# ALiBi's key part moved from the exponential's bias into the values, in a kernel of sliding-window attention and a swish feed-forward layer

## Chip, cores, metric

One core of a Trainium2 chip. The metric is device time in microseconds (us), the median of the runs, compared with runs of the kernel before on the same chip in the same rounds. Engines: PE is TensorE (matmul), ACT is ScalarE, DVE is VectorE, POOL is GpSimd, SP is SyncE. SBUF is the on-chip memory of the tiles, PSUM the one that the matmuls write. A run counts as slow when it is over 1.5% above the fastest of its kernel; slow ones are left out of every time and ratio here.

## The reference

```python
# q, k, v: (8 batches, 8 heads, 576 positions, 64); w_in: (512, 2048), w_out: (2048, 512)
scores = scale * np.matmul(q, k.transpose(0, 1, 3, 2))
rel = pos[:, None] - pos[None, :]
bias = slopes[:, None, None] * (-np.abs(rel))          # slopes: 2^-(h+1)
mask = (rel >= 0) & (rel < 128)
scores = np.where(mask, scores + bias[None], -1e9)
attn = softmax(scores)                                  # as exp, sum, divide
x = (attn @ v) as (8*576, 512)
h = x @ w_in
g = h * (1 / (1 + np.exp(-beta * h)))
out = g @ w_out
```

Inside the window the bias is −slope·(query − key). The query part cancels in the softmax, so what remains is a factor exp(slope·key) for each key and head. It can stand in the exponential's bias (before), in the values and in the column of ones that gives the row sum (the change). In 128-blocks of keys it has two versions, one for queries in the key's own block and one for queries in the next block.

## The kernel before

Scores are kept transposed, keys on partitions. In batches 2 to 7 one "visit" (`SC`) covers 1024 columns: two heads by 512. Four exponentials, each with its per-partition bias, one mask product on DVE, and then the PV matmuls (`PV`), whose values come from a tile that POOL casts from fp32.

```python
    def decayed(pt, sps, p, own, w):
        for e in range(2):
            h = 2 * p + e
            for half, cols in ((0, slice(0, own)), (1, slice(own, w))):
                nc.scalar.activation(
                    out=pt[:, e, cols], in_=sps[e][:, cols], func=ACTF.Exp,
                    scale=qscale, bias=bias[:, half, h : h + 1],
                )

    def SC(b, m, p):
        ...                                  # score matmuls into SS, 64 rows
        pt = pt_pool.tile([P, 2, 512], BF16, name="pt", tag="pt")
        decayed(pt, sps, p, OWN[m], 512)
        nc.vector.tensor_tensor(out=pt[:], in0=pt[:], in1=masks[m][:], op=ALU.mult)

    def cast_v(b, sb):                       # one block of values, POOL
        return nc.gpsimd.tensor_copy(
            out=VS[b % 2][0:rows, sb, :, 0:D], in_=fs.pop(("v", b, sb))[0:rows])

    def store():                             # results leave from POOL's queue
        row0, cols, o = waiting.pop(0)
        eng = nc.sync if row0 >= B * S - 2 * P else nc.gpsimd
        eng.dma_start(out=out[row0 : row0 + P, cols], in_=o)

    def Hm(g, j, cs):                        # feed-forward, first layer
        ...                                  # matmuls into hps (two PSUM buffers)
        nc.scalar.activation(out=sig[:], in_=hps, func=ACTF.Tanh, scale=beta_h[:, j : j + 1])
        nc.vector.scalar_tensor_tensor(
            out=gts[g][:, j, :], in0=sig[:], scalar=1.0, in1=hps, op0=ALU.add, op1=ALU.mult)
```

The last line writes gT and with it frees hps. So PE waits for DVE when DVE is late by more than the two hps buffers cover (8 waits, 4.1 us in this kernel's profile). In the traces of this kernel the operations of DVE follow one another, and so do POOL's (two neighbours overlap by at most 0.32 us on DVE and 0.08 on POOL): a mask that takes long delays the gT behind it. POOL carries the casts of q and k, the values, the loads of the weights and the stores.

The softmax here doesn't subtract the row's maximum and nothing guards it: scores larger than these inputs give would overflow.

## Time and profile before

| | kernel before |
|---|---|
| time, median | 339.4 us (338.2 to 340.5, 4 runs) |
| span of the profiled run | 336.8 us, granted PE clock 1.000 |
| mask of 1024 columns: mean, longest | 0.74 us, 1.21 us |
| PE waits over 0.7 us after the first 20 us | 7, together 5.7 us |

The prediction shows the lines of this profile that it used. The timeline: start, duration, engine, line, operation, output and inputs, shapes, count; in brackets the idle time before it and what ended that.

```profile
149.85 0.61 POOL L226 CAST vs<-fst 128x512 bf16<-128x512 f32 x1 [2.75 <-DMA fst<-in_v_dram]
152.02 0.61 POOL L226 CAST vs<-fst 128x512 bf16<-128x512 f32 x1 [1.55 <-DMA fst<-in_v_dram]
...
152.41 0.76 DVE L426 TENSOR_TENSOR pt<-pt,mask 128x1024 bf16<-128x1024 bf16 x1 [0.77 <-ACT pt L319]
...
154.57 0.69 DVE L426 TENSOR_TENSOR pt<-pt,mask 128x1024 bf16<-128x1024 bf16 x1 [0.77 <-ACT pt L319]
```

POOL waits for each tile to land (2.75 and 1.55 us here), so the casts are spread, and each mask finds POOL idle or nearly so (0.76 and 0.69 us).

### The profile page before, as it was taken

How to read it: one execution, taken by the hardware profiler on the slowest of the kernel's cores; microseconds unless marked ns; L12 is line 12 of the kernel's file. 1: busy time of each engine (PE TensorE's matmuls, PEld its weight loads, DVE VectorE, ACT ScalarE, POOL GpSimd, SP SyncE). 2: the span in 40 equal slices, each digit the busy share in tenths (PEclk: the TensorE clock that was granted, in tenths of full speed). 3: DMA queues.
4: the chain of work that ended last, by engine and by line, in shares of the span. 5: the costliest groups of instructions: out<-in, count | busy, mean ns of one | idle time of the engine just before them, and what ended most of it. 6: DMA issues, size and time to landing. Idle time of an engine off the chain costs nothing.

```text
span 336.8 us, 6208 instructions
## 1 busy us (share of the span) xinstructions
PE 320.8 (95%) x2293; PEld 155.4 (46%) x2293; DVE 200.0 (59%) x435; ACT 207.0 (61%) x405; POOL 103.5 (31%) x177
## 2 busy tenths in 40 slices
PE   8889899999998999999999999999999999999995
PEld 4545454444443454444444444444444444444444
DVE  6757897655468883766187717671778167525500
ACT  3767857565538875778469747774878465345511
POOL 4945630428345337321305142322100100010010
PEclk9999999999999999999999999999999999999999
DMA  7999999999999999991939986997120211210022
GB/s 201 241 283 224 168 201 216 202 197 256 215 224 250 176 217 253 219 201 35 219 80 193 186 200 145 214 161 173 45 58 15 78 47 49 55 64 31 0 85 73
DMA packets 146159, 51.81 MB, mean 154 GB/s; under 512 B 135360, under 2 KB 143824, under 8 KB 146128
## 3 DMA queue, kind: packets, MB, share of 16 engines
q1 hardware_dynamic: 139152, 38.29, 61.4%
q0 software_dynamic: 6944, 13.11, 16.4%
q8 instruction: 18, 0.29, 0.4%
q14 instruction: 13, 0.11, 0.1%
q10 hardware_dynamic: 32, 0.01, 0.0%
HBM read 36.71 MB, written 9.44 MB: 137 GB/s over the span
## 4 chain that ended last, share of the span: by engine, by line
PE 73%; DVE 13%; ACT 10%; issue 3%; DVEq 0%; ACTq 0%
PE ops L528 34%; PE hps L502 26%; ACT pt L319 7%; DVE gT L510 4%; PE SS L418 3%; DVE pt L426 3%; ACT sig L509 2%; PE pv L455 2%; PE hpo L502 2%; DVE qkT L252 1%; PE pv L451 1%; PE SS L103 1%; DVE xnp L337 1%; DVE xn L337 1%; PE SS L299 1%
## 5 line engine op out<-in xcount | busy, mean ns | idle before, releaser
L502 PE MATMUL hps<-XT,W 128*128 128x512 bf16 x540 | 135.2, 379 | 4.5 <-DVE gT L510 4.1
L528 PE MATMUL ops<-W,gT 128*128 128x512 bf16 (+1 forms) x592 | 138.5, 374 | 0.5 <-ACT osb L538 0.5
L510 DVE SCALAR_TENSOR_TENSOR gT<-sig,hps 128x512 bf16<-128x512 bf16 x135 | 91.2, 682 | 65.9 <-ACT sig L509 65.2
L509 ACT ACTIVATE sig<-hps,beta_h 128x512 bf16<-128x512 f32 x135 | 92.5, 695 | 56.3 <-PE hps L502 51.6
L319 ACT ACTIVATE pt<-SS,bias 128x256 bf16<-128x256 f32 (+1 forms) x192 | 75.0, 478 | 15.4 <-PE SS L418 15.4
L528 PEld LDWEIGHTS <-gT 128*128 128x128 bf16 x592 | 54.0, 98 | 57.7 <-issue 2.4
L502 PEld LDWEIGHTS <-W 128*128 128x128 bf16 x576 | 51.7, 98 | 60.5 <-issue 9.5
L545 POOL DMA_DIRECT2D out_dram<-osb x34 | 18.4, 542 | 114.0 <-ACT osb L538 113.8
L426 DVE TENSOR_TENSOR pt<-pt,mask 128x1024 bf16<-128x1024 bf16 x48 | 35.6, 742 | 26.6 <-ACT pt L319 26.5
L538 ACT ACTIVATE osb<-ops 128x512 f32<-128x512 f32 (+1 forms) x28 | 16.6, 592 | 38.3 <-PE ops L528 38.3
L226 POOL CAST vs<-fst 128x512 bf16<-128x512 f32 (+1 forms) x40 | 26.0, 657 | 34.3 <-DMA fst<-in_v_dram 31.2
L211 POOL CAST bst<-fst 128x512 bf16<-128x512 f32 (+1 forms) x32 | 20.7, 646 | 49.0 <-DMA fst<-in_q_dram 35.0
L337 DVE TENSOR_TENSOR xn<-pv,zs 128x256 bf16<-128x256 f32 (+1 forms) x62 | 25.9, 421 | 1.6
L212 POOL CAST bst<-fst 128x512 bf16<-128x512 f32 (+1 forms) x32 | 20.6, 644 | 18.1 <-DMA fst<-in_k_dram 17.9
L455 PE MATMUL pv<-vs,pt 128*128 128x65 bf16 x240 | 21.4, 193 | 0.0
L455 PEld LDWEIGHTS <-pt 128*128 128x128 bf16 x240 | 16.5, 97 | 8.4
L418 PE MATMUL SS<-qkT 64*128 64x256 bf16 (+2 forms) x240 | 18.9, 252 | 1.0 <-ACT pt L319 0.8
L418 PEld LDWEIGHTS <-qkT 64*128 64x128 bf16 x240 | 8.2, 94 | 21.2 <-issue 20.7
L451 PE MATMUL pv<-vs,pt 128*128 128x65 bf16 x192 | 17.9, 193 | 0.0
L451 PEld LDWEIGHTS <-pt 128*128 128x128 bf16 x192 | 15.2, 98 | 5.5
L536 DVE TENSOR_SCALAR osb<-ops 128x512 f32<-128x512 f32 (+1 forms) x9 | 5.9, 657 | 18.6 <-PE ops L528 18.5
L336 DVE RECIPROCAL zs<-pv 128x4 f32<-128x4 f32 (+1 forms) x66 | 11.3, 173 | 9.3 <-PE pv L455 8.2
(83 smaller groups left out, 176.5 us busy)
## 6 DMA issues: line engine op xcount, KB each, us to landing
out_dram<-osb POOLq DMA_DIRECT2D x34, 256.0 KB, 3.1
fst<-in_k_dram SPq DMA_DIRECT2D x32, 256.0 KB, 5.1
fst<-in_q_dram SPq DMA_DIRECT2D x32, 256.0 KB, 4.8
fst<-in_v_dram SPq DMA_DIRECT2D x32, 256.0 KB, 4.4
W<-in_moe_w_in_dram POOLq DMA_DIRECT2D x4, 512.0 KB, 7.3
W<-in_moe_w_out_dram POOLq DMA_DIRECT2D x4, 512.0 KB, 10.7
fst<-in_q_dram SPq DMA_DIRECT2D x8, 128.0 KB, 4.1
fst<-in_k_dram SPq DMA_DIRECT2D x8, 128.0 KB, 4.0
```

The source lines that it names most:

```text
L211: nc.gpsimd.tensor_copy(out=t[0:rows, 0], in_=fs.pop(("q", b, sb))[0:rows])
L226: return nc.gpsimd.tensor_copy(out=VS[b % 2][0:rows, sb, :, 0:D], in_=fs.pop(("v", b, sb))[0:rows])
L319: nc.scalar.activation(out=pt[:, e, cols], in_=sps[e][:, cols], func=ACTF.Exp, scale=qscale, bias=bias[:, half, h : h + 1],)
L337: nc.vector.tensor_tensor(out=xn, in0=pv[0:nq, :, 0:D], in1=zs[0:nq].broadcast_to([nq, 4, D]), op=ALU.mult)
L418: nc.tensor.matmul(o, lhsT=qk[64 * e : 64 * e + 64, 1, p, P * kb : P * kb + P], rhs=qk[64 * e : 64 * e + 64, 0, p, P * kb : P * kb + nq], ...
L426: nc.vector.tensor_tensor(out=pt[:], in0=pt[:], in1=masks[m][:], op=ALU.mult)
L451: nc.tensor.matmul(pv[:, hl, 0 : D + 1], lhsT=weights(b, qb - 1, h, 1), rhs=vs[:, qb - 1, h, 0 : D + 1], start=True, stop=False,)
L455: nc.tensor.matmul(pv[:, hl, 0 : D + 1], lhsT=weights(b, qb, h, 0), rhs=vs[:, qb, h, 0 : D + 1], start=qb == 0, stop=True,)
L502: nc.tensor.matmul(hps, lhsT=W1[:, c, bass.ts(j, P)], rhs=XT[:, c, c0 : c0 + TOKG], start=(c == 0), stop=(c == NDM - 1),)
L509: nc.scalar.activation(out=sig[:], in_=hps, func=ACTF.Tanh, scale=beta_h[:, j : j + 1])
L510: nc.vector.scalar_tensor_tensor(out=gts[g][:, j, :], in0=sig[:], scalar=1.0, in1=hps, op0=ALU.add, op1=ALU.mult)
L528: nc.tensor.matmul(ops_[:, cols], lhsT=gT[:, j, i * P : i * P + P], rhs=W2[:, j, cols], start=(j == 0), stop=(j == NFF - 1),)
```

## The change

Its intent: from batch 1 on the factor exp(slope·key) goes into the values. POOL's cast of a value block becomes a product that writes both versions (1024 columns in place of 512), the column of ones gets the factor too, and a visit needs one exponential without bias in place of four. The table matmuls of batch 1 fall away and masks take their place (a third one for the tail); batch 1's q copies go from DVE to ACT, and the mask set-up moves ahead on DVE. The core of the diff:

```diff
 def cast_v(b, sb):
-    return nc.gpsimd.tensor_copy(
-        out=VS[b % 2][0:rows, sb, :, 0:D], in_=fs.pop(("v", b, sb))[0:rows])
+    f = fs.pop(("v", b, sb))
+    if b == 0:
+        return nc.gpsimd.tensor_copy(out=VS0[0:rows, sb, :, 0:D], in_=f[0:rows])
+    x, w, n = f[0:rows], fall[0:rows], 2 if sb < 4 else 1
+    return nc.gpsimd.tensor_tensor(
+        out=VS[b % 2][0:rows, 2 * sb : 2 * sb + n, :, 0:D],
+        in0=bass.AP(tensor=x.tensor, offset=x.offset,
+                    ap=[list(x.ap[0]), [0, n], [D, H], [1, D]]),
+        in1=bass.AP(tensor=w.tensor, offset=w.offset,
+                    ap=[list(w.ap[0]), [H, n], [1, H], [0, D]]),
+        op=ALU.mult)
+
+def values(b, kb, h, then):
+    return VS0[:, kb, h, 0 : D + 1] if b == 0 else VS[b % 2][:, 2 * kb + then, h, 0 : D + 1]
 ...
 def SC(b, m, p):
-    decayed(pt, sps, p, OWN[m], 512)
+    nc.scalar.activation(out=pt[:], in_=SS[:], func=ACTF.Exp, scale=qscale)
     nc.vector.tensor_tensor(out=pt[:], in0=pt[:], in1=masks[m][:], op=ALU.mult)
 ...                      # batch 1 (SP_): the same; no table matmuls; SCT(1): a third mask
-FOUR = {1: 10, 2: 4}
+FOUR = {1: 10, 2: 8}     # hidden tiles that use the other PSUM buffers
 ...                      # set-up: fall = exp(bias), factors into the ones' column, two fills
```

More of the change, by code (lines that the diff above doesn't have):

```diff
@@ L63 @@
     table = const.tile([P, H, 3, P], BF16, name="table")
-    masks = [const.tile([P, 2, 512], BF16, name=f"mask{m}") for m in range(2)]
+    masks = [const.tile([P, 2, 512], BF16, name=f"mask{m}") for m in range(3)]
     kpos = const.tile([P, 1], F32, name="kpos")
@@ L67 @@
     PC = const.tile([P, 1024 + 64], BF16, name="pc")
-    VS = [const.tile([P, NQB, H, D + 2], BF16, name=f"vs{i}") for i in range(2)]
+    fall = const.tile([P, 2, H], F32, name="fall")
+    fallb = const.tile([P, 2, H], BF16, name="fallb")
+    VS0 = const.tile([P, NQB, H, D + 2], BF16, name="vs")
+    VS = [const.tile([P, 2 * NQB - 1, H, D + 2], BF16, name=f"vs{i}") for i in range(2)]
     QK = [const.tile([P, 2, NP, NQB * P], BF16, name=f"qkT{i}") for i in range(2)]
@@ L136, in ones, with padding, falls @@
     def ones():
+        nc.vector.memset(VS0[:, :, :, D : D + 1], 1.0)
+    def padding():
+        nc.gpsimd.memset(VS0[64:P, 4, :, 0:D], 0.0)
         for i in range(2):
-            nc.vector.memset(VS[i][:, :, :, D : D + 1], 1.0)
-    def padding():
-        for i in range(2):
-            nc.gpsimd.memset(VS[i][64:P, 4, :, 0:D], 0.0)
             nc.gpsimd.memset(QK[i][:, :, :, S:], 0.0)
+            nc.gpsimd.memset(VS[1 - i][64:P, 8, :, 0:D], 0.0)
         nc.gpsimd.memset(PC[:, 1024:], 0.0)
-    def biases():
+    def falls():
         for h in range(H):
@@ L152, in biases @@
                 )
+        nc.scalar.activation(out=fallb[:], in_=bias[:], func=ACTF.Exp)
+        nc.vector.tensor_copy(out=fall[:], in_=fallb[:])
+        for i in range(2):
+            w = fallb[:]
+            nc.vector.tensor_copy(
+                out=VS[i][:, 0:8, :, D : D + 1].rearrange("k (n a) h d -> k n (a h d)", a=2),
+                in_=bass.AP(tensor=w.tensor, offset=w.offset,
+                            ap=[list(w.ap[0]), [0, 4], [1, 2 * H]]))
+            nc.vector.tensor_copy(
+                out=VS[i][:, 8, :, D : D + 1].rearrange("k h d -> k (h d)"), in_=w[:, 0])
     def betas():
@@ L176, in tail_masks @@
         fill(1, 384, 1, P, ALU.is_lt)
+        fill(2, 0, 4, 64, ALU.is_ge)
+        fill(2, 256, 4, 64, ALU.is_lt)
     fs = {}
@@ L251, in TP @@
                     tok[:, c], lhsT=src[:, i, c], rhs=ident[:], start=True, stop=True)
-            (nc.vector.tensor_copy if b or i else nc.scalar.copy)(
+            (nc.vector.tensor_copy if i else nc.scalar.copy)(
                 out=QK[b % 2][:, i, p, 0:FULL], in_=tps[:])
@@ L270 @@
              "B": ((1, 256, 256, P), (2, 0, 256, 256), (3, 128, 384, P))}
-    PLAIN = ((1, "B"),)
     WIDTH = {"A": 384, "B": 512}
@@ L277, in SP_ @@
         w = WIDTH[vis]
-        plain = (b, vis) in PLAIN
+        plain = b == 1
         for e in range(2):
@@ L305, in SP_ @@
         pts[b, vis, p] = pt
-        if not plain:
-            nc.scalar.activation(
-                out=pt[:, :, 0:w], in_=sps[:, :, 0:w], func=ACTF.Exp, scale=qscale)
-            return
-        decayed(pt, [sps[:, e] for e in range(2)], p, 256, w)
-        nc.vector.tensor_tensor(
-            out=pt[:, :, 0:w], in0=pt[:, :, 0:w], in1=masks[0][:, :, 0:w], op=ALU.mult)
-    def decayed(pt, sps, p, own, w):
-        for e in range(2):
-            h = 2 * p + e
-            for half, cols in ((0, slice(0, own)), (1, slice(own, w))):
-                nc.scalar.activation(
-                    out=pt[:, e, cols], in_=sps[e][:, cols], func=ACTF.Exp,
-                    scale=qscale, bias=bias[:, half, h : h + 1],
-                )
+        nc.scalar.activation(out=pt[:, :, 0:w], in_=sps[:, :, 0:w], func=ACTF.Exp, scale=qscale)
+        if plain:
+            nc.vector.tensor_tensor(
+                out=pt[:, :, 0:w], in0=pt[:, :, 0:w], in1=masks[0][:, :, 0:w], op=ALU.mult)
     def room(b, shape, i):
@@ L340, in PVP @@
     def PVP(b, vis, p):
-        vs = VS[b % 2]
         if vis == "A":
@@ L353, in PVP @@
                         pv[:, 2 * n + e, 0 : D + 1], lhsT=pt[:, e, at : at + P],
-                        rhs=vs[:, kb, 2 * p + e, 0 : D + 1],
+                        rhs=values(b, kb, 2 * p + e, int(kb < q0 + n)),
                         start=i == 0, stop=i == len(ws) - 1,
@@ L369, in SCT @@
         for e in range(2):
+            if b:
+                break
             t = table[:, e]
@@ L381, in SCT @@
                         rhs=qk[64 * e : 64 * e + 64, 0, p, FULL:S],
-                        start=False, stop=True, skip_group_check=True,
+                        start=b > 0, stop=True, skip_group_check=True,
                     )
@@ L386, in SCT @@
             scale=qscale)
+        if b:
+            nc.vector.tensor_tensor(
+                out=PC[:, 0:1024], in0=PC[:, 0:1024],
+                in1=masks[2][:].rearrange("p e w -> p (e w)"), op=ALU.mult)
     def DT(b, sb):
@@ L401 @@
     COLS = {0: (0, 384), 1: (128, 256), 2: (0, 384), 3: (192, 320), 4: (128, None)}
-    OWN = (256, 320)
     def SC(b, m, p):
@@ L406, in SC @@
         qk = QK[b % 2]
-        sps = [SS[:, e] for e in range(2)]
         for kb in ((0, 1), (2, 4, 3))[m]:
@@ L411, in SC @@
             for e in range(2):
-                o = sps[e][:, at : at + min(nq, 512 - at)]
+                o = SS[:, e, at : at + min(nq, 512 - at)]
                 if kb in (0, 2):
@@ L439, in PV @@
         nq = ROWS[qb]
-        vs = VS[b % 2]
         if g == 0:
@@ L452, in PV @@
                     pv[:, hl, 0 : D + 1], lhsT=weights(b, qb - 1, h, 1),
-                    rhs=vs[:, qb - 1, h, 0 : D + 1], start=True, stop=False,
+                    rhs=values(b, qb - 1, h, 1), start=True, stop=False,
                 )
@@ L456, in PV @@
                 pv[:, hl, 0 : D + 1], lhsT=weights(b, qb, h, 0),
-                rhs=vs[:, qb, h, 0 : D + 1], start=qb == 0, stop=True,
+                rhs=values(b, qb, h, 0), start=qb == 0, stop=True,
             )
@@ L689, in tail_casts @@
             cast_v(b, 4)
+        falls()
+        constants_masks()
+        tail_masks()
         after(get_pair(1, 0), w1[0])
@@ L752, in open_o @@
                 tc.tile_pool(name="psum_o", bufs=2, space=bass.MemoryType.PSUM))
-        steps = [h[2], biases, constants_masks, h[3], R(0), h[4], A(0), h[5], B_(0), R(1), h[6],
+        steps = [h[2], h[3], R(0), h[4], A(0), h[5], B_(0), R(1), h[6],
                  A(1), B_(1), R(2), h[7], A(2), R(3), B_(2), A(3), h[8], B_(3), open_o, VA(0),
-                 h[9], VA(1), h[10], VA(2), tail_masks, lambda: TT(0), h[11], VA(3),
+                 h[9], VA(1), h[10], VA(2), lambda: TT(0), h[11], VA(3),
                  lambda: SCT(0), VB(0), h[12], VB(1), lambda: PV(0, 4, 0), VB(2), h[13], XO(0),
```

## The prediction

"Lock" stands in it for what the trace of the kernel before shows: a mask that begins inside a cast on POOL ends late. Of the 18 such masks 16 ended 0.54 to 0.64 us after the cast; the one at 168.46 ended 1.10 us after its cast and 0.55 after the next, and one in batch 1 (40.97) 0.94 us after. How long a product takes on POOL no trace had shown yet: the prediction's +5 to +8 us for DVE and its 150 us for POOL rest on an estimate of mine.

> **What bounds the kernel now.** I read the page's busy times and slices first, then the groups of instructions, then the waits, then the timeline round the places where TensorE (PE) stands still.
>
> ```profile
> PE 320.8 (95%) x2293; PEld 155.4 (46%) x2293; DVE 200.0 (59%) x435; ACT 207.0 (61%) x405; POOL 103.5 (31%) x177
> ...
> DVE gT L510 <- ACT sig L509: 67.2, 68, 7.7
> ACT sig L509 <- PE hps L502: 51.6, 81, 5.8
> ...
> PE hps L502 <- DVE gT L510: 4.1, 8, 0.8
> ...
> L319 ACT ACTIVATE pt<-SS,bias 128x256 bf16<-128x256 f32 (+1 forms) x192 | 75.0, 478 | 15.4 <-PE SS L418 15.4
> L426 DVE TENSOR_TENSOR pt<-pt,mask 128x1024 bf16<-128x1024 bf16 x48 | 35.6, 742 | 26.6 <-ACT pt L319 26.5
> L226 POOL CAST vs<-fst 128x512 bf16<-128x512 f32 (+1 forms) x40 | 26.0, 657 | 34.3 <-DMA fst<-in_v_dram 31.2
> L307 ACT ACTIVATE pt<-SX 128x1024 bf16<-128x1024 f32 x4 | 4.1, 1024 | 0.2
> L288 PE MATMUL SS<-table,ident 128*128 128x384 bf16 x16 | 4.0, 335 | 0.0
> ```
>
> The first line: PE is busy 95% of 336.8 us, ACT and DVE some 60%, so work taken from ACT is worth only what PE waits for it. Busy PE time hides short stalls (ends are modelled), so I went through the starts of the matmuls in the timeline. Two dense 128x512 matmuls start 216 ns apart, and a switch to or from the 64-row score matmuls costs about 95 ns more; what exceeds that I call stall. It sums to 22 us: 7.4 in the first 20 us, 5.0 from 20 to 40, 1.2 from 40 to 60 and about 8.6 from 60 to the end, 0.7 of it in the drain. The last 280 us are thus within 3% of what this order of matmuls allows. The waits say the same: PE waits for gT 8 times, 4.1 us together. The group lines give the costs used below. One such stall in the timeline:
>
> ```profile
> 166.87 1.56 ACT L319 ACTIVATE pt<-SS,bias 128x256 bf16<-128x256 f32 x4
> ...
> 167.95 0.61 POOL L211 CAST bst<-fst 128x512 bf16<-128x512 f32 x1
> ...
> 168.46 1.21 DVE L426 TENSOR_TENSOR pt<-pt,mask 128x1024 bf16<-128x1024 bf16 x1 [0.77 <-ACT pt L319]
> ...
> 168.51 0.61 POOL L212 CAST bst<-fst 128x512 bf16<-128x512 f32 x1
> ...
> 169.59 0.68 DVE L510 SCALAR_TENSOR_TENSOR gT<-sig,hps 128x512 bf16<-128x512 bf16 x1
> ...
> 170.32 1.02 PE L502 MATMUL hps<-XT,W 128*128 128x512 bf16 x4 [0.57 <-DVE gT L510]
> ```
>
> Four exponentials hold ACT for 1.56 us, the mask behind them takes 1.21 us instead of 0.69 because two casts on POOL lie over it, gT comes late, and PE waits for the PSUM buffer that gT frees. Nine stalls over 0.4 us, some 6.2 us together, stand between 104 and 281 us. Four of them (147.6, 169.6, 215.3, 223.3) follow a mask that took 0.97 to 1.21 us, that is, one that a POOL cast held up.
>
> [...]undisturbed masks take 0.69 us, and each one that starts inside a cast ends about 0.55 us after that cast. gT (one input in PSUM) stays at 0.68 us beside casts.
>
> **The change part by part.**
>
> *Exponentials.* The 48 visits of batches 2 to 7 have four ACTIVATEs each, 75.0 us / 48 = 1.56 us; one of 1024 columns takes 1.02. ACT saves 0.54 x 48 = 26 us, and another 0.54 x 4 = 2 us in batch 1. Four q copies of batch 1 move from DVE to ACT: +4 x 0.585 = +2.3 us. ACT goes from 207 to about 181 us. Nearly all of this lies beside PE work. On the path: each of the nine late stalls can shrink by at most the 0.54 us by which exp, and the tanh behind it, end earlier. The two at 104.4 and 107.7 (1.4 us) lie where the change also gives four more hidden tiles of group 2 another PSUM buffer. I take -4.0 us of the 6.2 for both together, before what POOL does.
>
> *PE.* The table matmuls go in batch 1: 4 visits x 2 of 384 columns and 2 of 512, at 216 ns per 512: 8 x 0.162 + 2 x 0.216 = 1.7 us. PE is the bound there, so all of it counts: -1.7 us. The 2283 matmuls left are the same. Of the qkT waits in batch 1 (0.42, 0.27 and 0.55 us of stall at 27.5, 31.7 and 36.6) the split of the copies over two engines takes perhaps half: -0.6 us. With the table matmuls gone, less work covers the rest.
>
> *DVE.* Off: 4 q copies of 0.685 = 2.7 us. On: 4 masks of 768 columns at about 0.55 us, one 1024-column mask for the tail at 0.69, five small copies (about 0.5) and two more mask fills (2 x 0.28). Busy time stays at 200 to 202 us plus what POOL blocks. But place matters: the order of instructions puts the small copies ahead of the second k copy of batch 0, and the fills ahead of the reciprocal and beta_h behind it. In the chain of the kernel before, these places are on the path (masks 7.98, qkT 9.20, zs 11.38, beta_h 12.02, PE 12.15). I count +1.0 us at the start.
>
> *POOL.* [...]It has idle time, so that is not the bound. It hurts in two ways. First the lock: I laid the products into the POOL timeline of before (each where its v tile had landed, the next behind it) and looked which masks start inside one. The delay of DVE comes to 9.7 us if DVE gets its turn between two POOL operations and 13.1 if it does not, against 4.7 and 5.3 with a length of 1.1 us: +5 to +8 us of DVE delay. In the stalls above, some half of a mask's delay reached PE: +2.5 to +4, I take +3.0. Second, the products of batch 1 stand before the W2 loads and batch 2's casts: W2's later loads go out some 3 us later, and batch 2's transposes wait for the last. The third of these landed at 70.9 us and the score matmuls that need it start at 71.1, so there is no slack: +0.5 us, with the chance of 2. Later batches have 4 us or more of slack for the values.
>
> The sum: -4.0 - 1.7 - 0.6 + 1.0 + 3.0 + 0.5 = -1.8 us. On 339.3 that is 337.5; the times of before scatter by 1.2 us each way. Since shorter exponentials also start the masks earlier, which helps in front of a POOL product that has not begun, I put it at 337.0.
>
> **The rivals.** (a) *ACT relief is worth more:* the nine stalls and the waits of batch 1 all vanish because one exponential frees the score tile and ACT together, and POOL's products turn out short (cast-like, about 1.2 us). Then -6.2 - 1.7 - 1.5 + 1.0 = -8.4: 331. For it: the waits name ACT's sig in 65 us of DVE's idle time. Against it: PE itself stalls for 8 us only, and the two-input operation reads twice as much. (b) *POOL takes the place of ACT:* the products run back to back, DVE's masks starve behind them for several us at a time, gT is late in every batch and PE stalls 1.5 us or more per batch: +9 on top, 346. For it: at 168.46 the second cast kept the lock although the mask had been waiting. Against it: v tiles land about 2 us apart, and only some 8 masks come per batch. (c) *Nothing moves:* all of ACT's saving lies beside PE, only the table matmuls count, and the start takes them back: 338 to 339.
>
> **Range and chances.** PE's work sets a floor: with all stalls after 20 us gone except those inherent to the small transposes, some 326 us, which nobody should expect. Rivals (a) and (b) mark the ends; I give each about one in ten. Predicted 337.0 us, range 331.5 to 343.0. Faster by over 2% (under 332.5) 0.13, slower by over 2% (over 346) 0.05, within 0.82.
>
> **What would show it.** Right: ACT near 181 us, 2283 matmuls, POOL near 150 us[...], masks (two SBUF inputs) lengthened to 1.5 us and more where they start inside a product, first 20 us about 1 us later at the same instruction, stalls of PE after 60 us no more than 2 us below before. Wrong: products near 1.2 us (the POOL term falls away and (a) gains), masks starved for over 3 us (b), or PE waiting at the first scores of batch 2 for over 1 us. If the time falls by more than 6 us, I have undervalued the relief of ACT on the path to gT; if it rises by more than 4, I have undervalued the lock.

## The result, and the profile after

The changed kernel takes 358.78 us (355.21 to 360.37, 4 runs) against 339.37: a ratio of 1.056, 95% interval 1.047 to 1.065. It is slower by 19 us, far outside the predicted range. Ratios here and below are the mean time of one kernel's runs over that of the other's of the same rounds, so they are not quite the ratio of the medians that I quote.

The page of the changed kernel, first the busy times, then the granted PE clock in 40 slices (tenths of full speed), then three groups (busy time, mean ns of one, idle time before them and what ended it):

```profile
PE 325.2 (91%) x2283; PEld 155.6 (44%) x2283; DVE 227.4 (64%) x442; ACT 182.7 (51%) x254; POOL 146.1 (41%) x178
...
PEclk9999989999998999995999999999989999999999
...
L445 DVE TENSOR_TENSOR pt<-pt,mask 128x1024 bf16<-128x1024 bf16 x48 | 56.7, 1181 | 23.1 <-ACT pt L444 23.0
...
L247 POOL TENSOR_TENSOR vs<-fst,fall 128x1024 bf16<-128x1024 f32 (+1 forms) x35 | 63.3, 1822 | 13.1 <-DMA fst<-in_v_dram 12.7
...
L444 ACT ACTIVATE pt<-SS 128x1024 bf16<-128x1024 f32 x48 | 48.9, 1019 | 22.9 <-PE SS L437 22.9
```

ACT is relieved as intended (207 to 183 us). But the mask, the same instruction as before, takes 1181 ns on average in place of 742. The waits of the changed kernel (engine, what it waited for; us in total, times, longest) say where it reaches PE:

```profile
POOL vs L247 <- DMA fst<-in_v_dram: 12.7, 11, 3.1
PE hps L520 <- DVE gT L528: 11.1, 4, 6.9
...
PE pv L469 <- DVE xn L353: 4.1, 2, 3.2
...
PE tpt L291 <- DVE xnp L353: 4.0, 1, 4.0
```

PE waited 4.1 us for gT before, in 8 waits of at most 0.8; now 11.1 us in 4 waits, the longest 6.9. The two other long waits of PE, for xn (3.2 us) and xnp (4.0 us), are also for DVE results that stood behind a long mask (5.14 us at 105.23, 4.91 us at 40.28). For a value tile PE hardly waits (0.2 us in all). The first line is a sign of the bunching below: POOL waited for value tiles 19 times, 31.2 us before, now 11 times, 12.7 us, so more tiles lie ready when POOL gets to them. The timeline of the longest stall:

```profile
154.25 0.54 POOL L563 DMA_DIRECT2D out_dram<-osb  x1 [7.08 <-ACT osb L556]
154.81 7.47 POOL L247 TENSOR_TENSOR vs<-fst,fall 128x1024 bf16<-128x1024 f32 x4
154.90 7.93 DVE L445 TENSOR_TENSOR pt<-pt,mask 128x1024 bf16<-128x1024 bf16 x1 [1.00 <-ACT pt L444]
156.31 0.29 PE L473 MATMUL pv<-vs,pt 128*128 128x65 bf16 x4
162.76 0.67 DVE L528 SCALAR_TENSOR_TENSOR gT<-sig,hps 128x512 bf16<-128x512 bf16 x1
163.48 3.57 PE L520 MATMUL hps<-XT,W 128*128 128x512 bf16 x8 [6.88 <-DVE gT L528]
```

Read it from the top. A store at the head of POOL's queue waits 7.08 us for its data; meanwhile four value tiles land. Then the four products run back to back for 7.47 us. The mask starts 0.09 us after the first and ends at 162.83, that is 0.55 us after the last product (162.28): it stood through all four. gT comes behind it, and PE has stood for 6.88 us. At a second place a mask stood through two products and the DMA issue on POOL between them, and ended 0.60 us after the second:

```profile
40.02 1.91 POOL L247 TENSOR_TENSOR vs<-fst,fall 128x1024 bf16<-128x1024 f32 x1
40.28 4.91 DVE L337 TENSOR_TENSOR pt<-pt,mask 128x1024 bf16<-128x1024 bf16 x1
41.86 0.80 POOL L267 DMA_DIRECT2D W<-in_moe_w_out_dram  x1
42.68 1.91 POOL L247 TENSOR_TENSOR vs<-fst,fall 128x1024 bf16<-128x1024 f32 x1
```

Not every mask that met a run stood through it. Four others in this trace (76.82, 78.97, 81.50 and 130.32; 1.19 to 1.51 us) ended 0.55 us after the product in which they had begun, though the next product had started 0.04 us before that end. The next product was then the longer one: 2.35 us at 77.48 and at 79.79 in place of 1.90, and 1.48 to 1.49 at 82.10 and 131.24 (64 rows) in place of 1.05.

There is a second cost that I had not thought of. The windows of the changed kernel (stretch; its length, busy time and number of instructions of PE, PEld, DVE, ACT, POOL; granted PE clock, DMA share, GB/s):

```profile
152.00:156.00 4.00, 4.00 (x28) 1.82 (x26) 2.48 (x3) 3.26 (x5) 1.73 (x2) 1.00 0.38 111
...
160.00:164.00 4.00, 0.52 (x2) 0.24 (x2) 4.00 (x4) 0.00 (x0) 2.27 (x2) 0.50 0.00 0
164.00:168.00 4.00, 4.00 (x16) 1.24 (x15) 1.82 (x6) 1.59 (x3) 0.00 (x0) 0.50 0.21 44
```

After the stall the granted PE clock is 0.50: the eight hps matmuls at 163.48 take 3.57 us, while eight took 1.90 at 153.58. Windows at or near 0.50 follow each of the four stalls of over 3 us in this trace (41.5: 4.05 us; 108.0: 3.38; 156.4: 7.05; 253.7: 3.24). In windows of 1 us, PE's busy time times (1 − clock) sums to 7.8 us here and to 0.0 in the kernel before. That is the most that the half clock can have cost in matmuls. By the starts of the matmuls, the stretches at half clock run 6.5 us over the full pace; part of it is won back elsewhere (the net is in the sum further down).

### The profile page after: what moved, and what is told of

It reads as the page before. It is cut to its first block, busy times and chain, and to the rows that moved or that the text cites.

```text
span 356.6 us, 6044 instructions
## 1 busy us (share of the span) xinstructions
PE 325.2 (91%) x2283; PEld 155.6 (44%) x2283; DVE 227.4 (64%) x442; ACT 182.7 (51%) x254; POOL 146.1 (41%) x178
## 4 chain that ended last, share of the span: by engine, by line
PE 76%; DVE 15%; ACT 5%; issue 2%; DVEq 0%; ACTq 0%
PE ops L546 34%; PE hps L520 28%; DVE pt L445 6%; PE SS L437 4%; DVE gT L528 3%; ACT pt L444 2%; DVE pt L337 2%; PE pv L473 2%; PE hpo L520 2%; PE pv L469 1%; PE SS L106 1%; ACT sig L527 1%; ACT pt L335 1%; PE tps L280 1%; DVE xnp L353 1%
## 5 line engine op out<-in xcount | busy, mean ns | idle before, releaser
L520 PE MATMUL hps<-XT,W 128*128 128x512 bf16 x532 | 136.1, 387 | 11.2 <-DVE gT L528 11.1
L546 PE MATMUL ops<-W,gT 128*128 128x512 bf16 (+1 forms) x592 | 140.2, 377 | 1.4 <-DVE osb L554 0.9
L527 ACT ACTIVATE sig<-hps,beta_h 128x512 bf16<-128x512 f32 x133 | 91.4, 688 | 86.5 <-PE hps L520 74.0
L445 DVE TENSOR_TENSOR pt<-pt,mask 128x1024 bf16<-128x1024 bf16 x48 | 56.7, 1181 | 23.1 <-ACT pt L444 23.0
L247 POOL TENSOR_TENSOR vs<-fst,fall 128x1024 bf16<-128x1024 f32 (+1 forms) x35 | 63.3, 1822 | 13.1 <-DMA fst<-in_v_dram 12.7
L444 ACT ACTIVATE pt<-SS 128x1024 bf16<-128x1024 f32 x48 | 48.9, 1019 | 22.9 <-PE SS L437 22.9
L229 POOL CAST bst<-fst 128x512 bf16<-128x512 f32 (+1 forms) x32 | 21.2, 663 | 11.6 <-DMA fst<-in_k_dram 11.6
L469 PE MATMUL pv<-vs,pt 128*128 128x65 bf16 x192 | 18.3, 194 | 4.1 <-DVE xn L353 4.1
L473 PE MATMUL pv<-vs,pt 128*128 128x65 bf16 x240 | 21.8, 195 | 0.0
L437 PEld LDWEIGHTS <-qkT 64*128 64x128 bf16 x240 | 8.1, 95 | 21.6 <-issue 21.2
L235 POOL CAST bst<-fst 128x512 bf16<-128x512 f32 x16 | 10.0, 640 | 6.8 <-PE xtp L378 3.6
```

The lines of the kernel that those rows point to most:

```text
L229: return nc.gpsimd.tensor_copy(out=t[0:rows, 1], in_=fs.pop(("k", b, sb))[0:rows])
L247: return nc.gpsimd.tensor_tensor(out=VS[b % 2][0:rows, 2 * sb : 2 * sb + n, :, 0:D], in0=bass.AP(tensor=x.tensor, offset=x.offset, ap=[lis ...
L437: nc.tensor.matmul(o, lhsT=qk[64 * e : 64 * e + 64, 1, p, P * kb : P * kb + P], rhs=qk[64 * e : 64 * e + 64, 0, p, P * kb : P * kb + nq], ...
L444: nc.scalar.activation(out=pt[:], in_=SS[:], func=ACTF.Exp, scale=qscale)
L469: nc.tensor.matmul(pv[:, hl, 0 : D + 1], lhsT=weights(b, qb - 1, h, 1), rhs=values(b, qb - 1, h, 1), start=True, stop=False,)
L473: nc.tensor.matmul(pv[:, hl, 0 : D + 1], lhsT=weights(b, qb, h, 0), rhs=values(b, qb, h, 0), start=qb == 0, stop=True,)
```

## The experiments

Theory L (lock): a mask, two inputs from SBUF, that begins inside a POOL operation with an input from SBUF does not end before it, and may be held on through the next ones if they follow without a gap (7.93 us above); so the loss is a matter of how long POOL's runs of reading operations are. Rival R1: POOL's time as such, values late for PV, or the rest of the change (start, other PSUM buffers, batch 1). Rival R2: the size of one product alone counts, the lock falling at each end of an instruction. Seventeen kernels ran.

| run | what | time, us | ratio to before [95%] |
|---|---|---|---|
| e1_cast_only | after, plain cast of V (wrong result) | 335.08 | 0.992 [0.988, 0.996] |
| e2_before_products | before, products by 1 on POOL | 354.99 | 1.049 [1.044, 1.053] |
| e7_reduce | after, mask replaced by a one-input DVE operation (wrong) | 344.66 | 1.017 [1.013, 1.021] |
| e4_split | after, each product in two halves | 351.17 | 1.036 [1.029, 1.043] |
| e3_one_input | after, copies in place of products (wrong) | 341.53 | 1.002 [0.995, 1.009] |
| e6_dve_product | after, products on DVE | 367.28 | 1.082 [1.075, 1.088] |
| e5_act_store | after, stores from ACT's queue | 349.42 | 1.029 [1.024, 1.033] |
| e12_before_act_store | before, stores from ACT's queue | 352.17 | 1.039 [1.035, 1.044] |
| e14_gap_memset | after, memsets ahead of each product | 346.96 | 1.024 [1.021, 1.027] |
| e15_turns | after, each product waits for the mask before it | 344.28 | 1.014 [1.008, 1.020] |
| e18_turns_gap | e15, and e14's memsets in batch 1 | 341.10 | 1.005 [1.001, 1.009] |
| e8_fold | factor in the masks, plain V | 342.52 | 1.012 [1.010, 1.014] |
| e10_fold_pool | e8, set-up on POOL | 361.78 | 1.066 [1.062, 1.070] |
| e11_fold_pool_act_store | e10, stores from ACT's queue | 366.87 | 1.081 [1.078, 1.085] |
| e13_fold_late | before to batch 1, folded from batch 2 | 342.47 | 1.011 [1.009, 1.013] |
| e16_fold_spread | e13, set-up spread | 334.90 | 0.989 [0.986, 0.992] |
| e17_fold_turns | e16, and V casts wait for the mask before them | 334.49 | 0.987 [0.984, 0.990] |

### Take the products away, and add them alone (e1, e2)

```diff
 # e1: the changed kernel
-    x, w, n = ...;  return nc.gpsimd.tensor_tensor(out=VS[b % 2][... both versions ...], ...)
+    return nc.gpsimd.tensor_copy(out=VS[b % 2][0:rows, 2 * sb, :, 0:D], in_=f[0:rows])
 # e2: the kernel before, from batch 1 on
-    return nc.gpsimd.tensor_copy(out=VS[b % 2][0:rows, sb, :, 0:D], in_=...)
+    ... the changed kernel's product with two versions, by a tile of ones
```

> The changed kernel with the cast of the values on POOL as before (one version, unscaled, read for both uses): wrong result on purpose, everything else as changed. Theory L[...]: without products the masks go back to about 0.74 us on average and the time falls to 333 to 336 us, a little below before, since one exponential per visit and 1.7 us of table matmuls remain as gains. Theory S (the loss is in the new set-up work, the order of DVE's first instructions, and the masks added in batch 1): stays at 350 us or more. Theory E (one long exponential in place of four makes ACT or the score tile worse): stays at 350 or more, with long waits on ACT.

> The kernel before with only the products added: each v cast of batches 1 to 7 becomes the same two-version product on POOL, with factors of one, so the result stays right; exponentials with bias, tables and set-up stay as before. Theory L: slower than before by about what the changed kernel lost to masks, 352 to 362 us, with masks of 4 us and more and PE stalls of 3 us and more right after them. Theories S and E: 338 to 341 us, as before.

Measured: e1 335.08 us, 0.8% faster than before, with the wrong values. e2 354.99 us, 4.9% slower than before, with a right result and with all four exponentials, tables and PSUM buffers of before (from two runs; its profiled run was slow). So the product on POOL alone makes the loss, and everything else in the change is worth about −3 us. That dismisses the second half of R1. The group lines of e1's page:

```profile
L438 DVE TENSOR_TENSOR pt<-pt,mask 128x1024 bf16<-128x1024 bf16 x48 | 39.3, 820 | 25.4 <-ACT pt L437 25.1
...
L246 POOL CAST vs<-fst 128x512 bf16<-128x512 f32 (+1 forms) x35 | 23.5, 676 | 36.2 <-DMA fst<-in_v_dram 29.6
```

With the cast back, the masks are at 820 ns, and POOL waits for value tiles for 29.6 us again, as before the change.

### A DVE operation with one input (e7)

```diff
-    nc.vector.tensor_tensor(out=pt[:], in0=pt[:], in1=masks[m][:], op=ALU.mult)
+    nc.vector.tensor_reduce(out=pt[:, 0, 0:1], in_=pt[:].rearrange("p e w -> p (e w)"),
+                            op=ALU.max, axis=mybir.AxisListType.X)
```

> The changed kernel with each of the 48 mask products of batches 2 to 7 replaced by a reduction of the same 1024 columns on DVE, which has one SBUF input (wrong result on purpose). It is longer by itself[...]. POOL's products stay. Theory L, by the two SBUF inputs of the mask: none of these 48 is stretched by POOL, stalls of over 3 us after 60 us are gone, and the time falls to 340 to 347 us in spite of the longer instruction (batch 1's masks still starve). A rival, load: DVE and POOL simply have too much to do; then the time rises above 359.

Measured: 344.66 us. From its page:

```profile
L445 DVE TENSOR_REDUCE pt<-pt 128x1 bf16<-128x1024 bf16 x48 | 58.6, 1221 | 18.8 <-ACT pt L444 18.3
...
L247 POOL TENSOR_TENSOR vs<-fst,fall 128x1024 bf16<-128x1024 f32 (+1 forms) x35 | 60.6, 1744 | 15.9 <-DMA fst<-in_v_dram 15.5
```

The products are all there, and they do not touch the reductions: the 31 that overlap a reading POOL operation take 1.20 to 1.22 us, the 17 others 1.22. DVE is as busy as in the changed kernel (227.8 against 227.4 us), since the reduction is slower than an undisturbed mask (1.22 against 0.69 us). And yet no stall of PE after 60 us is over 1.3 us, where the changed kernel has three over 3. So what does the harm is the mask meeting POOL's operations, not DVE's busy time and not late values, which dismisses the first half of R1. The reduction differs from the mask in two ways, one input and hardly any output; that it is the input, against POOL's reads, is my reading of two more facts: gT, which writes 512 columns but reads one input from SBUF, takes 0.65 to 0.69 us in the changed kernel beside a reading POOL operation (57 cases) as elsewhere, and in e14 a mask goes on beside POOL operations that only write. (Its 2.5 us stall at 43.7 falls in batch 1, whose eight masks I had left as they were.)

### Half-size products, and one-input copies (e4, e3)

```diff
 # e4
-    nc.gpsimd.tensor_tensor(out=both versions, in0=x twice, in1=w, op=ALU.mult)   # 1024 columns
+    for n in range(2 if sb < 4 else 1):
+        r = nc.gpsimd.tensor_tensor(out=version n, in0=x, in1=w[n], op=ALU.mult)  # 512 columns
 # e3
+    nc.gpsimd.tensor_copy(out=both versions, in_=x twice)
```

> The changed kernel with each two-version product as two one-version products (about 1.05 us each, right result). If DVE gets its turn at the end of each POOL instruction, the longest wait of a mask is halved and the time falls to 345 to 352 us. If a mask goes on waiting as long as POOL's next instruction is ready (starvation, what the 4.9 to 7.9 us masks of the changed kernel suggest), nothing is gained: 354 to 364 us, with masks of 5 us and more.

> The changed kernel with each product on POOL replaced by a copy that reads the v tile twice and writes the same 1024 columns (one input, wrong result on purpose). Estimate from the 0.61 us of a 512-column cast: 1.1 to 1.2 us instead of 1.9. If the runs of POOL work are what starves the masks, shorter instructions leave more gaps between the arrivals of v tiles: masks stretched to 3 us at most, 338 to 346 us. If only two-input instructions on POOL lock the masks out: as with the plain cast, 333 to 336 us. If the length does not matter but the number of columns written does: 355 or more.

e4: 351.17 us, inside what was expected if the lock falls at the end of each instruction, so by its time alone e4 would speak for R2. The timeline of e4 decides otherwise:

```profile
149.62 6.03 POOL L248 TENSOR_TENSOR vs<-fst,fall 128x512 bf16<-128x512 f32 x6
...
149.71 6.49 DVE L445 TENSOR_TENSOR pt<-pt,mask 128x1024 bf16<-128x1024 bf16 x1 [1.00 <-ACT pt L444]
```

Six products of about 1 us, one mask through all six; it ends at 156.20, 0.55 us after the sixth. Here the ends of five products did not free the mask, which dismisses R2 with its lock that falls at each end. What e4 gains lies elsewhere: the stall at 108 us is gone, the longest falls from 7.05 to 5.61 us, and the one at 41.5 us from 4.05 to 2.06, where a mask that began at 40.49 ended at 43.41, 1.14 us after a product, while the next one ran; between the two lay a DMA issue (42.20 to 43.01), and that the mask got in during it is my reading. e3: 341.53 us (wrong; its profiled run slow). The copy of 1024 columns takes 1.07 us on average in place of 1.98, and the time is that of before within the interval. Its longest mask was still 4.42 us, across a run of four copies. So products, copies and casts (168.46 in the kernel before) have all held masks, and what differs is how long the runs last.

### Somewhere else for the product, and for the stores (e6, e5, e12)

```diff
 # e6
-    return nc.gpsimd.tensor_tensor(out=VS[b % 2]...
+    return nc.vector.tensor_tensor(out=VS[b % 2]...
 # e5 (changed kernel) and e12 (kernel before)
-    eng = nc.sync if row0 >= B * S - 2 * P else nc.gpsimd
+    eng = nc.sync if row0 >= B * S - 2 * P else nc.scalar
```

> The changed kernel with the products on DVE itself, in order with the masks (right result). [...]DVE's busy time goes from about 200 (without blocks) to 235 to 240 us, POOL has no v work from batch 1 on. Theory L: no mask stands behind POOL products; but products delay gT by 1.2 us in DVE's order: 338 to 346 us. Load as the cause: 355 or more.

> The changed kernel with the stores of the result issued from ACT's queue and not POOL's (right result). In the changed kernel the longest run of products (154.8 to 162.3 us) began when a store at POOL's head, waiting for its output tile, let go, with the v tiles long landed. If such bunching makes the longest runs, the stalls of 7.0 us at 156 and 3.2 us at 254 shrink to under 1.5 us and the time falls by 7 to 12 us, to 346 to 352. If the products bunch anyway (POOL too slow for v tiles 2 us apart): 355 to 360.

> The kernel before with the stores on ACT's queue alone, as a control for the run of the changed kernel with ACT stores, which gained 9 us. With casts of 0.6 us bunching costs little: 336 to 340 us, within 1% of before. If stores on POOL were costly by themselves, it would gain the same 9 us: 330. Right result.

e6 missed: 367.28 us, worse than the changed kernel; by its expectation that would mean load, but the trace shows waiting. A product, 1.23 us on average on DVE, waits there for its tile: 19.9 us in 11 waits for the V tiles, up to 7.9 us, in which neither masks nor gT go on. DVE's busy time is 239.0 us. The run does not speak on the lock. e5: 349.42 us, 9 us less than the changed kernel; the stalls at 156 and 254 us, each behind a store at POOL's head, are gone, those at 40 and 109 us remain. That supports the reading of the bunching. But e12, the control, missed: the same move costs the kernel before 13 us (one stall of 6.4 us at 78.4; DVE waits up to 6.9 us for an exponential, and that ACT held it behind stores whose data were not ready is my reading, not shown). So e5's 9 us is a net figure, and moving the stores is no cure.

### Give the mask a gap, or a turn (e14, e15, e18)

If a next operation that is always ready is the harm, then a gap, or a wait that gives DVE its turn, must cure it with all the work left in place.

```diff
 # e14: ahead of each product (e18: in batch 1 only)
+    for _ in range(6):
+        nc.gpsimd.memset(scrap[:], 0.0)          # 128 columns; reads no SBUF
 # e15, e18: the product waits for the mask issued last before it
+    if "mask" in late:
+        after(r, late["mask"])                   # a dependency
 ...
-    nc.vector.tensor_tensor(out=pt[:], in0=pt[:], in1=masks[m][:], op=ALU.mult)
+    late["mask"] = nc.vector.tensor_tensor(out=pt[:], in0=pt[:], in1=masks[m][:], op=ALU.mult)
```

> The changed kernel, with six small memsets of 128 columns on GpSimd ahead of each V product from the second batch on: GpSimd operations that read no tensor in SBUF, as a gap of some 0.5 us or more between two products. Correct result expected. Lock with no gap (the mask needs one moment in which no GpSimd operation is reading, and gets none while the next product is ready): the longest masks end within the gap after the product that they met, so no mask over 2.0 + 0.7 = 2.7 us, against 7.93 in the changed kernel, the stalls of over 3 us fall to under 2, time 342 to 352. Plain loss of bandwidth while GpSimd is busy with anything, or a grant that only the emptying of GpSimd's queue gives: masks stay at 5 us or more, time 357 to 364.

> The changed kernel, with each V product made to wait for the mask that was issued last before it in the program's order, so that DVE gets a turn before each product; all else equal, the same work. Correct result expected. Starvation by a product that is always ready: masks of over 3 us vanish except where two products follow the same mask, the stalls of over 3 us after 40 us go with them, time 338 to 347. If the time is lost in GpSimd's busy time itself (4 us of work more in each batch, whatever its order), the wait only moves it: 355 to 362. If the wait delays products until PV matmuls stand for V: 350 to 370, with PE waits on vs in place of gT.

> e15 (each V product waits for the mask issued last before it), and in the second batch alone the six memsets of e14 ahead of each product, because there two products wait for the same mask and the second starved one mask in e15 (5.47 us at 39.6, stall 4.67 us, half clock after it). Correct result expected. If that one stall is most of what e15 still lost: it vanishes, no mask over 3 us in the second batch, 337 to 341. If the wait for masks itself costs the rest: 343 to 345 as in e15.

e14: 346.96 us with 43 us of memsets on top (POOL is busy for 185 us against 146), with a right result. Its timeline:

```profile
159.50 1.53 POOL L249 MEMSET scrap<- 128x128 bf16 x6
161.00 1.90 POOL L250 TENSOR_TENSOR vs<-fst,fall 128x1024 bf16<-128x1024 f32 x1
161.57 1.88 DVE L448 TENSOR_TENSOR pt<-pt,mask 128x1024 bf16<-128x1024 bf16 x1 [0.23 <-ACT pt L447]
162.84 1.51 POOL L249 MEMSET scrap<- 128x128 bf16 x6
```

The mask meets the product, and ends at 163.45, 0.55 us after it (162.90), in the middle of the memsets. The longest mask is 3.07 us, at 89.12, a little over the 2.7 that I had expected; it stands in a run of q and k casts, which have no memsets between them. What e14 still loses is partly POOL's delay: its largest stall, 4.4 us at 126.9, waits for qkT, the transposed q and k of the next batch, whose casts presumably come late behind the longer products.

e15: 344.28 us, three quarters of the loss gone with the same work as the changed kernel and a few waits more. At the place of the 7.93 us mask its timeline has

```profile
154.85 0.54 POOL L566 DMA_DIRECT2D out_dram<-osb  x1 [5.39 <-ACT osb L559]
155.50 0.69 DVE L448 TENSOR_TENSOR pt<-pt,mask 128x1024 bf16<-128x1024 bf16 x1 [1.00 <-ACT pt L447]
156.33 3.76 POOL L247 TENSOR_TENSOR vs<-fst,fall 128x1024 bf16<-128x1024 f32 x2 [0.94 <-PE pv L476]
```

The store comes late as before, but the mask goes first, in 0.69 us, and the products follow. One stall of 4.67 us was left, at 41.0, where a mask of 5.47 us stood through two products of batch 1 that wait for the same earlier mask; the wait cannot part those. e18 puts memsets there as well: the stall is gone, no mask is over 3 us (the longest is 2.96, in a run of casts at 87), and the time is 341.10 us, at the edge of the expected 337 to 341. Of the 5.6% loss 5.1 points are undone by turns and gaps, with every product still on POOL.

### The factor in the masks (e8, e10, e11, e13, e16, e17)

This asks whether the gain of the exponentials can be had without a product on POOL. The factor of a key is multiplied into the mask, so there are eight masks (two kinds by four pairs of heads) in place of two; V stays a plain cast. It costs 32 small DVE operations once.

```diff
 # e13, e16, e17: the kernel before up to batch 1; from batch 2 on
+    def folded(m, p, j):
+        own = (256, 320)[m]
+        for e in range(2):
+            for half, cols in ((0, slice(0, own)), (1, slice(own, 512))):
+                r = nc.vector.tensor_scalar_mul(
+                    FM[m][p][:, e, cols], masks[m][:, e, cols],
+                    fall[:, half, 2 * p + e : 2 * p + e + 1])
+                after(r, ...)                    # not before a given gT (m = 0)
 ...
-        decayed(pt, sps, p, OWN[m], 512)
-        nc.vector.tensor_tensor(out=pt[:], in0=pt[:], in1=masks[m][:], op=ALU.mult)
+        nc.scalar.activation(out=pt[:], in_=SS[:], func=ACTF.Exp, scale=qscale)
+        nc.vector.tensor_tensor(out=pt[:], in0=pt[:], in1=FM[m][p][:], op=ALU.mult)
 # e16: the second set built pair by pair, behind the first four masks of batch 2
+        if (b, m) == (2, 0):
+            folded(1, p, None)
 # e17: cast_v also waits for the last mask, as the product in e15
 # e8: folded from batch 1 on, all set-up on DVE; e10: that set-up on POOL;
 # e11: e10 with the stores from ACT's queue
```

> A way to the change's aim without products: ALiBi's key part is multiplied into the 0/1 masks once, one mask per pair of heads, so the visit keeps one exponential and one mask product, no tables from batch 1 on, and the values are cast as before. Right result. Theory L: masks at about 0.74 us, 332 to 336 us. About 48 small DVE instructions at the start may cost 1 to 2 us of that. Theory E: 345 or more.

> The kernel with the key part folded into the masks, but with the set-up of masks and factors moved from DVE to POOL, in program order where POOL waited for DMA (after the paddings, after batch 1's first v casts, and ahead of batch 2's casts). In the first fold kernel the set-up stood ahead of qkT copies, beta_h and the reciprocals on DVE and PE stalled 18.5 us in the first 40 us against 12.4 in the kernel before; after 60 us it stalled about 4.7 us against 8. If only the place of the set-up spoilt it: first 40 us at 11 to 12 us of stall, 329 to 333 us, faster than before by 2 to 3%. If the small POOL instructions delay the q and k casts instead: 335 or more. Right result.

> The same with the stores of the result on ACT's queue. If a store waiting at POOL's head still bunches casts (masks of 1 us and more behind casts): 1 to 2 us less than the same kernel with stores on POOL. If the issue of stores costs ACT as much: the same within 1 us. Right result.

> The kernel before up to batch 1, tables and all; from batch 2 on the key part is folded into the masks (one exponential and one mask product per visit, plain values, casts on POOL as before). The 32 small instructions that build the folded masks are held back on DVE until the last gT tiles of the second token group, where DVE had idle time, so the start is that of before. If only the place of the set-up spoilt the first two fold kernels: stalls of the first 60 us as before (about 13 us), after that about 5 against 8.8, and 3 to 5 us less in all: 334 to 336.5 us, ratio 0.985 to 0.992. If the building delays gT around 66 to 76 us: 337 to 340. Right result.

> The kernel before up to the second batch, from the third batch the key part folded into eight sets of masks (no product on GpSimd, one exponential and one mask per visit), as e13, but the set-up of the second set is spread, one pair of heads behind each of the masks of the third batch, in place of one run of twelve operations at 77 us. Correct result expected. If e13's 1.1% loss was its bunched set-up (4.2 us of PE stall at 77 us): 334 to 339, ratio 0.985 to 1.0. If a run of four V casts on GpSimd that starves the masks is what is left: 339 to 342 with masks of 2.5 to 3 us at 90 and 154 us.

> e16 with each V cast made to wait for the mask issued last before it. Correct result expected. If runs of casts starve masks there: 1 to 2 us less than e16 and no mask over 2 us after 80 us. If those long masks cost PE nothing: the same as e16 within 0.5 us.

e8 (342.52 us) and e13 (342.47) are 1% slower than before, though no product is on POOL: e8 builds its masks in the first 60 us, where DVE is on the path, and e13 has twelve of the set-up operations in one run at 77 us, in front of an eviction that PE waits 4.2 us for. e10 and e11 missed badly (361.78, 366.87): POOL took about 1 us for a `tensor_scalar` of some 256 columns with a per-partition factor (mean of the 24 of one group 954 ns), its casts came late behind them, and PE stood for 8.3 and 10.6 us. e16 spreads the set-up and gives 334.90, with no stall over 1.1 us after 20 us; e17's waits add nothing that shows (334.49; the intervals overlap). From e17's page:

```profile
PE 317.8 (95%) x2253; PEld 155.2 (47%) x2293; DVE 209.5 (63%) x467; ACT 183.1 (55%) x262; POOL 104.4 (31%) x177
...
L443 DVE TENSOR_TENSOR pt<-pt,fm 128x1024 bf16<-128x1024 bf16 x42 | 32.0, 762 | 18.3 <-ACT pt L442 18.1
```

ACT is as much relieved as in the changed kernel, masks take 762 ns, and the kernel is correct and beats both: 1.3% under before. (Forty matmul records are missing from the traces of e10 to e12 and e14 to e18, 2253 of 2293 here, so sums of stalls are not compared with them.)

## Why the prediction was wrong

Its terms, one by one:

- *Counts and durations* were right or near: 2283 matmuls, ACT 182.7 us (predicted 181), POOL 146.1 (near 150). A product took 1.90 us undisturbed, less than my estimate of it, so its length is not what went wrong.
- *Start, +1.0*: stalls in the first 20 us went from 7.4 to 8.2. Right in size.
- *Exponentials −4.0, tables −1.7, qkT −0.6*, with the start −5.3: e1, which has all of it and no products, measures 335.08 against 338.75, −3.7 us (−2.9 by its ratio). The direction is right, the size too large by some 2 us. How it splits into the three terms was not tested.
- *Entry of batch 2, +0.5, with the chance of 2*: between 60 and 80 us no stall of the changed kernel is over 1 us.
- *Lock, +3.0.* This is the step that failed, by 13 to 21 us: products against plain casts are 358.78 against 335.08, 24 us (on the kernel before e2 gives 16; why these two differ was not tested). The lock was named rightly. Two reasons for its small size failed, and a cost was not seen.

The first reason was rival (b)'s "Against it: v tiles land about 2 us apart", so products would not run back to back. I had laid products into the timeline of before. But that timeline was the one in which POOL waited for tiles. In the changed kernel POOL comes late to them, above all behind a store that waits for PE's results, the tiles lie ready, and the products run three and four in a row (252 and 155 us); at 40 and 105 us two products with a DMA issue between them, and at 105 two casts behind, make the run. The stall then delays the next results and with them the store. This closing of the loop is my reading of the timeline; e5 supports it, as the stalls behind stores go when the stores leave the queue.

The second was the size of the delay: I took 5 to 8 us more of it for DVE (with the estimated length of a product), and "some half" of that for PE. The masks' time above 0.70 us went from 3.2 us before to 28.7, by 25.5. (My base was off too: I subtracted 4.7 and 5.3 us, for operations of 1.1 us, where the masks of before had lost 3.2.) And the half came from masks of 0.97 to 1.21 us. Short delays were partly hidden there, by the two hps buffers as I read it, but of a mask of 7.93 us nearly all reaches PE (6.88). The sum of the delays is therefore the wrong measure: in e14 the masks still lose 23.5 us, but none is over 3.07 us, and the kernel is 12 us faster than the changed one.

The cost not seen is the half clock. Each of the four long stalls was followed by some 3 us or more at or near a granted clock of 0.50, worth at most 7.8 us together.

In sum: against e1, waits of PE over 0.7 us after the first 20 us grew from 1.5 to 21.2 us and the smaller excess, where the slowed matmuls fall, from 10.5 to 14.6; together 23.8, against a span longer by 23.5 (356.6 and 333.1).

The prediction's own test, "if it rises by more than 4, I have undervalued the lock" and "masks starved for over 3 us (b)", named what then came. I gave it one chance in ten on an argument taken from the old timeline, though that timeline had the handing on of the lock in it (168.46, "the second cast kept the lock"). What stays open: why some masks stood on through the next POOL operations (7.93 us) and others ended 0.55 us after the first (the four from 76.82 on), and why the DMA issue of 0.80 us at 41.86 did not let the mask in while the memsets of e14 did, and one issue in e4 seems to have done so. An issue alone did not hold up the mask at 90.64 in the changed kernel, which began inside that of a store and took 0.69 us. No run here separates these.

## What to carry to other kernels

Before lengthening an operation on an engine whose operations hold up another's (here masks, for up to 7.93 us), don't lay the longer operation into the old timeline: ask what the engine will find ready once it runs late, since the transfers that spaced its work out may then do so no more (POOL's waits for value tiles fell from 31.2 to 12.7 us). If a victim starves behind a run of operations, look at order before size: a dependency that gives it a turn (e15) undid three quarters of a 5.6% loss without removing any work. Look at the longest delay, not at the sum (e14: 23.5 us of delay, none of its masks over 3.07 us, 12 us faster). And put a factor that is constant over the whole kernel into an operand that is already there (the mask, e16), with its set-up spread where the engine has time, rather than into work that recurs for each tile.

## What the runs show of the hardware

- Masks beside POOL. A mask stood for 7.93 us through four products, 6.49 through six of about 1 us (e4), 4.91 through two products and the DMA issue between them (0.80 us); each ended 0.55 to 0.60 us after the last product. Four masks of the changed kernel that also met products without a gap ended 0.55 us after the first (1.19 to 1.51 us). With memsets behind the product the mask ended 0.55 us after it, while they ran (e14). A `tensor_reduce` of 1024 columns took 1.20 to 1.22 us beside POOL's reads and 1.22 without them (e7). A mask that started first held up POOL: at 238.85 in the changed kernel it took 0.69 us, and the product that began 0.09 us after it 2.36 in place of 1.90. But in e15 the mask at 39.58 began 0.29 us before a product, while a DMA issue on POOL ran, and stood for 5.47 us. With a turn made for it by a dependency, the mask at 155.50 took 0.69 us (e15).
- Operations on POOL. A product of 1024 columns (fp32 and a broadcast fp32 factor, bf16 out) took 1.90 us undisturbed, one of 512 columns 1.05 (64 rows). A `tensor_scalar` with a per-partition factor took about 1 us for 256 bf16 columns (e10).
- PE's clock. The granted clock fell to 0.50 after waits of 3.2 to 7.1 us in the changed kernel. A wait of only 2.00 us, from 78.24 in e18, was followed by 0.50 as well (from 80.27, for 3.4 us), and eight matmuls took 3.57 us in place of 1.90.
